# Spreading filler matmuls, moving casts and halving the first transposes in an attention and MLP kernel

## Chip, cores, metric

One core of a Trainium2 chip. The metric is the device time of one execution in microseconds (us).

## The reference

```python
x = A_x                                    # 1 x 2048 x 512, bf16
xn = _layernorm(x)
q = xn @ wq                                # 32 heads of 128
k, v = last 512 rows of k_cache, v_cache   # 8 kv heads, each for 4 q heads
o = softmax(q @ k.T * 128**-0.5) @ v       # no mask
s = o @ wo                                 # 4096 -> 512
g = silu(silu(xn @ w1) @ w2)               # 512 -> 1792 -> 512
return x + s * g
```

## The kernel before

The 2048 tokens are worked in 4 blocks of 512, and each block in 32 steps, one per head: 128 steps, numbered s. In step s TensorE computes four score tiles for head s, q for head s + 2 and P times V for head s - 4. Block 0 fills the rest of each step with the MLP matmuls of all four blocks ("fillers"), blocks 1 to 3 with the output projection of the block before. The last projection is done in a tail with fewer, combined products. Every engine's order is the program's order. A **unit** is a group of matmuls that sum into one bank of PSUM, the memory that TensorE writes to here; ScalarE or VectorE has to read the bank out before the next unit can use it. Fillers that stand together between two other matmuls are called a **clump**.

```python
PS_BUFS = {"sc": 4, "q": 1, "o": 1, "f": 2}        # PSUM banks

# MLP unit: 4 matmuls into one of the two f banks, then tanh on ACT, then one pass on DVE
if c == 0:
    cur["ps"] = ps.tile([P, BLK], FP32, name="h_ps", tag=tag_of(f), bufs=PS_BUFS[tag_of(f)])
h_mm(cur["ps"], b, f, c, 0, BLK)
if c == ND - 1:
    h_evac(cur["ps"], b, f)        # th = tanh(0.5 h) on ACT; hT = (th + 1) * h on DVE

# q: one bank, emptied by a cast
if b == NBLK - 1 and h % 2 == 1:
    nc.scalar.copy(qT[s], cur["ps"])
else:
    nc.vector.tensor_copy(qT[s], cur["ps"])

# P V: one bank, emptied on DVE
cur["ps"] = ps.tile([P, BLK], FP32, name="o_ps", tag="o", bufs=1)

# one step
cut = spread(n)                    # how many fillers at each of six places
score(s, 0)
if s >= 1:
    normalise(s - 1, 2, 3)
    flip(s - 1)
for u in qu[:2]: u()
pump(cut[0])
for u in qu[2:]: u()
pump(cut[1])
score(s, 1)
for u in pu[:2]: u()
pump(cut[2])
for u in pu[2:]: u()
pump(cut[3])
score(s, 2)
normalise(s, 0, 1)
pump(cut[4])
score(s, 3)
pump(cut[5])
# then, one tile per step: stats of blocks 2 and 3 in steps 2-5 and 8-11,
# centring and transposing them in steps 7-10 and 14-17
...
# start: layer norm of tiles 0 and 1, then PE transposes
stats(0, 0); stats(0, 1)
rstd_first(0); center(0, 0); rstd_first(1); center(0, 1)
nc.scalar.activation(scratch, scratch, ACT.Tanh)      # loads the tanh table
warm_up(10)
t0 = turn(0); keep(nc.vector, t0, 0); warm_up(1)
t1 = turn(1); keep(nc.vector, t1, 1); warm_up(1)
```

(Line breaks of short loops are joined here.)

The softmax here doesn't subtract the row's maximum and nothing guards it: scores larger than these inputs give would overflow.

Of the kernel before, what the change touches and what calls it, by code (L numbers as in the profile page):

```python
# [9 lines left out]
P = 128  # L10
ALU = mybir.AluOpType
# [11 lines left out]
def kernel(  # L23
# [28 lines left out]
    FH = NFC // 2  # L52
    HALF = BLK // 2
    HP = HQ // 2

    x2 = A_x.flatten_outer_dims()
    out2 = out.flatten_outer_dims()
# [145 lines left out]
    def q_units(s, tag="q"):  # L203
        b, h = divmod(s, HQ)
        cur = {}

        def mm(c):
            if c == 0:
                cur["ps"] = ps.tile([P, BLK], FP32, name="q_ps", tag=tag, bufs=1)
            nc.tensor.matmul(  # L210
                cur["ps"],
                wq_sb[h // REP][:, c, (h % REP) * DH : (h % REP + 1) * DH],
                xnT[b][:, c, :],
                start=(c == 0),
                stop=(c == ND - 1),
            )
            if c == ND - 1:
                qT[s] = work.tile([P, BLK], BF16, name="qT", bufs=3)
                if b == NBLK - 1 and h % 2 == 1:
                    nc.scalar.copy(qT[s], cur["ps"])  # L220
                else:
                    nc.vector.tensor_copy(qT[s], cur["ps"])  # L222

        return [lambda c=c: mm(c) for c in range(ND)]
# [40 lines left out]
            out=s25[p].rearrange("p a b -> p (a b)"), in0=o[:, 0, :], in1=o[:, 1, :], op=ALU.add  # L265
        )

    def pv_units(s):
        b, h = divmod(s, HQ)
        cur = {}  # L270

        def mm(kc):
            if kc == 0:
                cur["ps"] = ps.tile([P, BLK], FP32, name="o_ps", tag="o", bufs=1)
            nc.tensor.matmul(  # L275
                cur["ps"], v_sb[h // REP][:, kc, :], pT[s][:, kc, :], start=(kc == 0), stop=(kc == NKC - 1)
            )
            if kc == NKC - 1:
                if s % 2 == 0:
                    oT[s // 2] = work.tile([P, 2, BLK], BF16, name="oT", tag="oT", bufs=OT_BUFS // 2)  # L280
                nc.vector.tensor_copy(oT[s // 2][:, s % 2, :], cur["ps"])  # L281
                if b == NBLK - 1 and s % 2 == 1:
                    row_sums(h // 2)
                del pT[s], p_all[s], qT[s], den[s]

        return [lambda kc=kc: mm(kc) for kc in range(NKC)]
# [38 lines left out]
    def out_units(b):  # L325
        acc = {}
        xes = {}

        def mm(j, h):
            t = b * BLKT + j  # L330
            if h == 0:
                acc[j] = ps.tile([P, D], FP32, name="s_ps", tag="f", bufs=2)
            nc.tensor.matmul(  # L333
                acc[j],
                oT[(b * HQ + h) // 2][:, h % 2, j * P : (j + 1) * P],
                wo_of(h),
                start=(h == 0),
                stop=(h == HQ - 1),
            )
            if h == HQ // 2:  # L340
                xes[j] = reg.tile([P, D], BF16, name="x_e", tag=f"pair{4 + j % 2}")
                nc.gpsimd.dma_start(xes[j], x2[ds(t * P, P), :])
            if h == HQ - 1:
                xe = xes[j]
                sg = reg.tile([P, D], FP32, name="sg", tag=f"pair{2 + j % 2}")
                nc.vector.tensor_tensor(out=sg, in0=acc[j], in1=g_sb[b][:, j, :], op=ALU.mult)
                nc.vector.scalar_tensor_tensor(  # L347
                    out=xe, in0=sg, scalar=0.25, in1=xe, op0=ALU.mult, op1=ALU.add
                )
                nc.gpsimd.dma_start(out2[ds(t * P, P), :], xe)  # L350

        return [lambda a=a: mm(*a) for a in out_order()]



# [76 lines left out]
    def tail():  # L432
# [42 lines left out]
        def bank(tag, shape, name):  # L475
            return ps.tile(shape, FP32, name=name, tag=tag, bufs=PS_BUFS[tag])
# [44 lines left out]
        for t in range(2):  # L521
            group(3, t, "sc")
            run(3, t, EARLY)
            for u in pv_units(NSTEP - LAG + t):
                u()
            for p in range(3 * t, 3 * t + 3):
                diag(p)
# [10 lines left out]
            run(5, t, EARLY)  # L538
        for p in range(8):
            skew(p)  # L540
        for u in pv_units(NSTEP - 1):
            u()
        for p in (14, 15):
            diag(p)
# [4 lines left out]
        for t in range(2):  # L549
            run(4, t, (HP - 2,))  # L550
            run(5, t, (HP - 2,))
        m2 = bank("q", [P, 2, HALF], "m2_ps")
        for p in EARLY:
            mm(m2[:, 0, :], 2, p, 0)
        for t in range(2):
# [54 lines left out]
    with tc.manual_schedule(engines={ENG.PE, ENG.Activation, ENG.DVE, ENG.SP, ENG.Pool}):  # L610
# [21 lines left out]
        def warm_up(n):  # L632
            for _ in range(n):
                nc.tensor.matmul(warm_ps, warm[:, 0:P], warm, start=True, stop=True)

        def turn(j):
            t_ps = ps.tile([P, ND, P], BF16, name="t_ps", tag="qo"[j % 2], bufs=1)
            for c in range(ND):
                nc.tensor.transpose(t_ps[:, c, :], x_blk[0][:, j, c * P : (c + 1) * P], ident)
            return t_ps  # L640

        def keep(eng, t_ps, j):
            dst = xnT[0][:, :, j * P : (j + 1) * P]
            (nc.scalar.copy if eng is nc.scalar else nc.vector.tensor_copy)(dst, t_ps)

        stats(0, 0)
        stats(0, 1)
        rstd_first(0)
        center(0, 0)
        rstd_first(1)  # L650
        center(0, 1)
        nc.scalar.activation(scratch, scratch, ACT.Tanh)
        warm_up(10)
        t0 = turn(0)
        keep(nc.vector, t0, 0)
        warm_up(1)
        t1 = turn(1)
        keep(nc.vector, t1, 1)
        warm_up(1)
        stats(0, 2)  # L660
        stats(0, 3)
        rstd_of(2, 2)
# [26 lines left out]
        for i in range(2 * FH):  # L689
            h_pair(i, i // FH)  # L690
            if i == 3:
                t2 = turn(2)
                t3 = turn(3)
                keep(nc.scalar, t2, 2)
                keep(nc.vector, t3, 3)
            if i >= 2 * FH - 4:
                stats(1, i - 2 * FH + 4)
            if i in (2 * FH - 3, 2 * FH - 2):
                k = i - 2 * FH + 3
                for u in q_units(k, "qo"[k]):  # L700
                    u()
# [26 lines left out]
        }  # L728
        sums = col_sums()

        def spread(n):

            cut = [n // 6] * 6
            for k in (5, 4, 1, 3, 0, 2)[: n % 6]:
                cut[k] += 1
            return cut if n != 4 else (0, 0, 0, 0, 2, 2)

        n_more = 4 * LAG
        wo_first = False
        for s in range(NSTEP):  # L740
            b, h = divmod(s, HQ)
            if b >= 1 and h == 0:
                assert done >= n_mlp or b > 1
                fill += out_units(b - 1)
            n = 4
            if b == 0:
                n = min(4 * (h + 1), n_more) + (h + 1) * (n_mlp - n_more) // HQ - done
            cut = spread(n)
            qu = q_units(s + 2) if s + 2 < NSTEP else []
            pu = pv_units(s - LAG) if s >= LAG else []  # L750
            score(s, 0)
            if s >= 1:
                normalise(s - 1, 2, 3)
                flip(s - 1)
            for u in qu[:2]:
                u()
            pump(cut[0])
            for u in qu[2:]:
                u()
            pump(cut[1])  # L760
            score(s, 1)
            for u in pu[:2]:
                u()
            pump(cut[2])
            for u in pu[2:]:
                u()
            pump(cut[3])
            score(s, 2)
            normalise(s, 0, 1)
            pump(cut[4])  # L770
            score(s, 3)
            if s == NSTEP - 1:
                normalise(s, 2, 3)
                flip(s)
            pump(cut[5])
            while sums and sums[0][0] <= s:
                sums.pop(0)[1]()
            for b2, s0 in ((2, 2), (3, 8)):
                if s0 <= s < s0 + BLKT:
                    stats(b2, s - s0)  # L780
                if s == s0 + BLKT - 1:
                    rstd_of(b2 * BLKT, BLKT)
            if s < 2:
                for j in (2 * s, 2 * s + 1):
                    center(1, j)
                    flip_x(1, j)
            for b2, s0 in ((2, 7), (3, 14)):
                if s0 <= s < s0 + BLKT:
                    center(b2, s - s0)
                    flip_x(b2, s - s0)  # L790
            if s % REP == 1 and s < HQ and s // REP + 2 < HKV:
                load_kq(s // REP + 2)
                load_v(s // REP + 2)
            if not wo_first and done >= n_mlp - BLKT * NFC:
                new_wo("big0")
                new_wo("big1")
                wo_first = True
            if s == HQ:
                for tag in ("big2", "big3", "pair0", "pair1"):
                    new_wo(tag)  # L800
            for args in wo_plan.get(s, []):
                load_wo(*args)
# [29 lines left out]
```

## Time and profile before

Before the change: 552.18 us, median of 4 runs (551.7 to 552.33). In the profile PE is TensorE, PEld its weight loads, DVE is VectorE, ACT is ScalarE and POOL is GpSimd. The page of the profiled run: the span; then busy time of each engine, its share of the span and its instructions; then the chain of work that ended last.

```profile
span 550.0 us, 8480 instructions
...
PE 541.0 (98%) x2628; PEld 261.6 (48%) x2676; DVE 458.5 (83%) x1261; ACT 389.0 (71%) x1122; POOL 20.6 (4%) x41
...
PE 93%; DVE 3%; ACT 1%; issue 1%; DMA 1%
```

TensorE is the bound. (48 of its 2676 matmul records are missing in this trace.) But "98%" cannot tell what is left, since the ends of matmuls are modelled and overlap. The starts can: back to back, 128x512 matmuls start 0.216 us apart and 128x256 ones 0.109 us. The Trainium skill ("TensorE: Matmul & The Clock Gate", Part 1) gives N / 2.4 GHz + 2.5 ns, which agrees. The program has 2324, 336 and 16 matmuls of 512, 256 and 128 columns; at that spacing they take some 539.4 us. **A slot**, in what follows, is one spacing of 0.216 us, and **a hole** is how much later than the spacing a matmul starts.

The view of waits, TensorE's alone (engine, line, what it waited for, us in total, times, longest):

```profile
PE warm_ps L634 <- DVE eps L73: 1.2, 1, 1.2
PE q_ps L210 <- DVE qT L222: 0.7, 1, 0.7
PE h_ps L676 <- DVE xnT L644: 0.3, 1, 0.3
PE o_ps L275 <- DVE oT L281: 0.2, 1, 0.2
PE t_ps L639 <- DVE x L122: 0.2, 1, 0.2
```

This view counts from the modelled end of the matmul before, which lies 0.16 us after the next start that was due (0.38 against 0.216 us), so it shows 0.65 us of a hole of 0.81, and the 0.11 us that it leaves of a hole of 0.28 is not listed at all. The starts show 0.81 us at q_ps, 0.36 us at o_ps, and in block 0 a further 1.5 us at h_ps and oB_ps, none of which is in the list. One of those, in the timeline (start, duration, engine, line, operation, count, and in brackets the idle time before and what ended it):

```profile
148.92 0.59 PE L146 MATMUL h_ps<-xnT,w 128*128 128x512 bf16 x2
149.34 0.60 ACT L156 ACTIVATE th<-h_ps 128x512 bf16<-128x512 f32 x1 [0.61 <-PE h_ps L146]
149.57 0.59 PE L146 MATMUL h_ps<-xnT,w 128*128 128x512 bf16 x2
149.97 0.69 DVE L157 SCALAR_TENSOR_TENSOR hT<-th,h_ps 128x512 bf16<-128x512 bf16 x1 [0.15 <-ACT th L156]
150.22 0.87 PE L146 MATMUL h_ps<-xnT,w 128*128 128x512 bf16 x2
```

Two back-to-back matmuls show 0.59 us together; the last pair shows 0.87, so its second one came 0.28 us late, at 150.71. It is the first matmul of a unit and needs the bank that the matmul at 148.92 filled last. Tanh and the DVE pass follow each other without queueing, and the bank is free at 150.66. The round trip of a bank, from the start of its last matmul to its next use, is thus 150.71 - 148.92 = 1.79 us. In between lie seven slots of 0.216 us, 1.51 us, because fillers come in pairs at the end of a step. The difference is the hole.

### The profile page before, as it was taken

Reading aid. Unit: us, or ns where it says so; the run is one execution under the profiler, and the core shown is the slowest. Engines: PE = TensorE matmul, PEld = TensorE weight load, DVE = VectorE, ACT = ScalarE, POOL = GpSimd, SP = SyncE. Lnnn points to the kernel's source line nnn. Section 1 sums busy time; section 2 is a strip of 40 time slices with the busy share of each in tenths; the row PEclk is TensorE's granted clock in tenths of the full one; section 3 lists DMA queues with packets and bytes.
Section 4 is the critical chain, followed back from the end, with each engine's and each line's share of the span. In section 5 each row is a group of like instructions: output and inputs, shape, how many; then the busy total and the mean of one; then the engine's idle time right before and its main releaser. Section 6 shows DMA issues by size and latency. Waiting matters only on the chain.

```text
span 550.0 us, 8480 instructions
## 1 busy us (share of the span) xinstructions
PE 541.0 (98%) x2628; PEld 261.6 (48%) x2676; DVE 458.5 (83%) x1261; ACT 389.0 (71%) x1122; POOL 20.6 (4%) x41
## 2 busy tenths in 40 slices
PE   8999999999999999999999999999999999999997
PEld 5644444444444444444444444444444444444586
DVE  6869978976886688898889888988898889988887
ACT  4658756766775677777777777777788888788600
POOL 1000100000000100010001000100010000000010
PEclk9999999999999999999999999999999999999999
DMA  9969779769749799979887988798879877987921
GB/s 286 250 114 182 155 152 153 155 144 178 147 79 204 161 214 223 205 147 189 164 151 145 189 164 144 155 188 161 153 150 184 156 150 152 183 153 154 172 78 39
DMA packets 297837, 89.69 MB, mean 163 GB/s; under 512 B 282304, under 2 KB 296896, under 8 KB 297792
## 3 DMA queue, kind: packets, MB, share of 16 engines
q1 hardware_dynamic: 296064, 85.09, 77.9%
q0 software_dynamic: 1312, 3.67, 2.7%
q8 instruction: 21, 0.34, 0.2%
q10 hardware_dynamic: 416, 0.39, 0.2%
q14 instruction: 24, 0.20, 0.1%
HBM read 17.30 MB, written 2.10 MB: 35 GB/s over the span
## 4 chain that ended last, share of the span: by engine, by line
PE 93%; DVE 3%; ACT 1%; issue 1%; DMA 1%
PE sc_ps L232 19%; PE q_ps L210 19%; PE o_ps L275 19%; PE s_ps L333 14%; PE oB_ps L179 9%; PE h_ps L146 6%; PE m_ps L473 4%; PE h_ps L676 2%; DVE p_all L247 1%; ACT p_all L235 1%; ACT th L156 1%; DMA x<-in_A_x_dram 1%; DVE oT L281 0%; DVE hT L157 0%; DVE x_e L347 0%
## 5 line engine op out<-in xcount | busy, mean ns | idle before, releaser
L235 ACT ACTIVATE p_all<-sc_ps 128x512 bf16<-128x512 f32 x512 | 305.4, 597 | 104.0 <-PE sc_ps L232 102.0
L232 PE MATMUL sc_ps<-kT,qT 128*128 128x512 bf16 x512 | 193.7, 379 | 0.7
L247 DVE TENSOR_SCALAR p_all<-p_all,rden 128x512 bf16<-128x512 bf16 x512 | 157.9, 351 | 9.1
L210 PE MATMUL q_ps<-xnT,wq 128*128 128x512 bf16 x498 | 134.4, 379 | 1.1 <-DVE qT L222 0.7
L275 PE MATMUL o_ps<-pT,v 128*128 128x512 bf16 x496 | 133.6, 379 | 0.7 <-DVE oT L281 0.2
L281 DVE CAST oT<-o_ps 128x512 bf16<-128x512 f32 x128 | 88.3, 689 | 41.2 <-PE o_ps L275 38.7
L235 ACT ACTIVATION_READ_ACCUMULATOR p_all<-sc_ps 128x1 f32 x512 | 100.7, 197 | 0.0
L333 PE MATMUL s_ps<-wo_big,oT 128*128 128x512 bf16 x327 | 98.0, 379 | 0.5
L232 PEld LDWEIGHTS <-qT 128*128 128x128 bf16 x512 | 50.1, 98 | 61.3 <-issue 1.4
L210 PEld LDWEIGHTS <-wq 128*128 128x128 bf16 x512 | 50.1, 98 | 60.9 <-issue 1.2
L275 PEld LDWEIGHTS <-v 128*128 128x128 bf16 x512 | 50.1, 98 | 59.9 <-issue 0.4
L222 DVE CAST qT<-q_ps 128x512 bf16<-128x512 f32 x112 | 76.9, 687 | 1.6 <-PE q_ps L210 1.1
L179 PE MATMUL oB_ps<-w,hT 128*128 128x512 bf16 x220 | 64.6, 379 | 0.3
L333 PEld LDWEIGHTS <-oT 128*128 128x128 bf16 x384 | 37.6, 98 | 45.3
L146 PE MATMUL h_ps<-xnT,w 128*128 128x512 bf16 x164 | 50.1, 379 | 0.6
L245 DVE RECIPROCAL rden<-den 128x2 f32<-128x2 f32 x256 | 40.4, 158 | 10.8 <-ACT p_all L235 10.8
L179 PEld LDWEIGHTS <-hT 128*128 128x128 bf16 x224 | 21.9, 98 | 26.4
L157 DVE SCALAR_TENSOR_TENSOR hT<-th,h_ps 128x512 bf16<-128x512 bf16 x42 | 28.7, 683 | 4.6 <-ACT th L156 4.6
L156 ACT ACTIVATE th<-h_ps 128x512 bf16<-128x512 f32 x42 | 25.1, 598 | 9.1 <-PE h_ps L146 9.1
L146 PEld LDWEIGHTS <-w 128*128 128x128 bf16 x168 | 16.4, 98 | 20.2 <-issue 0.7
L189 DVE SCALAR_TENSOR_TENSOR gate<-th,oB_ps 128x512 bf16<-128x512 bf16 x16 | 11.0, 687 | 13.8 <-ACT th L188 13.8
L350 POOL DMA_DIRECT2D out_dram<-x_e x12 | 6.6, 549 | 314.5 <-DVE rden L245 258.2
(63 smaller groups left out, 235.9 us busy)
## 6 DMA issues: line engine op xcount, KB each, us to landing
wq<-in_A_wq_dram SPq DMA_DIRECT2D x8, 512.0 KB, 4.3
w<-in_B_w_dram SPq DMA_DIRECT2D x3, 896.0 KB, 9.9
pT<-p_all SPq DMA_TRANSPOSE x128, 4.4
wo_big<-in_A_wo_dram SPq DMA_DIRECT2D x4, 512.0 KB, 4.6
x<-in_A_x_dram SPq DMA_DIRECT2D x3, 512.0 KB, 8.6
wo_big<-in_A_wo_dram SPq DMA_DIRECT2D x4, 384.0 KB, 4.6
x_e<-in_A_x_dram POOLq DMA_DIRECT2D x12, 128.0 KB, 3.0
out_dram<-x_e POOLq DMA_DIRECT2D x12, 128.0 KB, 2.2
```

The source lines that it names most:

```text
L146: nc.tensor.matmul(h_ps[:, lo : lo + n], w1_sb[f // FH][:, c, (f % FH) * P : (f % FH + 1) * P], xnT[b][:, c, lo : lo + n], start=(c == 0), ...
L156: nc.scalar.activation(th, h_ps, ACT.Tanh, scale=0.5)
L179: nc.tensor.matmul(cur["ps"], hT[b][f // 2][:, f % 2, j * P : (j + 1) * P], w2_sb[f // FH][:, f % FH, :], start=(f == 0), stop=(f == NFC - 1),
L210: nc.tensor.matmul(cur["ps"], wq_sb[h // REP][:, c, (h % REP) * DH : (h % REP + 1) * DH], xnT[b][:, c, :], start=(c == 0), stop=(c == ND - 1),
L222: nc.vector.tensor_copy(qT[s], cur["ps"])
L232: nc.tensor.matmul(sc, qT[s][:, j * P : (j + 1) * P], kT[h // REP], start=True, stop=True)
L235: nc.scalar.activation(p_all[s][:, :, j, :], sc.rearrange("p (kc q) -> p kc q", q=P), ACT.Exp, scale=INV_SQRT_DH, accum_out=den[s][:, j : ...
L245: nc.vector.reciprocal(rden, den[s][:, j0 : j1 + 1])
L247: nc.vector.tensor_scalar_mul(p_all[s][:, :, j, :], p_all[s][:, :, j, :], rden[:, j - j0 : j - j0 + 1])
L275: nc.tensor.matmul(cur["ps"], v_sb[h // REP][:, kc, :], pT[s][:, kc, :], start=(kc == 0), stop=(kc == NKC - 1))
L281: nc.vector.tensor_copy(oT[s // 2][:, s % 2, :], cur["ps"])
L333: nc.tensor.matmul(acc[j], oT[(b * HQ + h) // 2][:, h % 2, j * P : (j + 1) * P], wo_of(h), start=(h == 0), stop=(h == HQ - 1),)
```

## The change

It makes the tile order of TensorE smoother and takes single waits away. The matmuls are the same. Its core:

```diff
 # q cast of the last block
-                if b == NBLK - 1 and h % 2 == 1:
+                if b == NBLK - 1 and (h % 2 == 1 or h in busy):
                     nc.scalar.copy(qT[s], cur["ps"])
+    busy = {i // 4 + 3 for i, (_, h) in enumerate(out_order()) if h == HQ - 1}
 # tail: P V sums take turns between two banks
-            for u in pv_units(NSTEP - LAG + t):
+            for u in pv_units(NSTEP - LAG + t, "oq"[t]):
-        for u in pv_units(NSTEP - 1):
+        for u in pv_units(NSTEP - 1, "q"):
-        m2 = bank("q", [P, 2, HALF], "m2_ps")
+        m2 = bank("o", [P, 2, HALF], "m2_ps")
 # start: halves, tile 0 copied by ACT, tanh table later
-        center(0, 0)
+        center_half(0, 0)
+        center_half(0, 1)
         rstd_first(1)
-        center(0, 1)
-        nc.scalar.activation(scratch, scratch, ACT.Tanh)
+        center_half(1, 0)
+        center_half(1, 1)
         warm_up(10)
-        t0 = turn(0)
-        keep(nc.vector, t0, 0)
-        warm_up(1)
-        t1 = turn(1)
-        keep(nc.vector, t1, 1)
-        warm_up(1)
+        for j in range(2):
+            for k in range(2):
+                turn_half(j, k)
+                keep_half(nc.vector.tensor_copy if j else nc.scalar.copy, j, k)
+                if k:
+                    warm_up(1)
+        nc.scalar.activation(scratch, scratch, ACT.Tanh)
 # block 0: one filler after each other unit (blocks 1 to 3 keep their order)
+                units = S[0:1] + qu + S[1:2] + pu[:2] + S[2:3] + pu[2:] + S[3:4]
+                for i, u in enumerate(units):
+                    u()
+                    pump((i + 1) * n // len(units) - i * n // len(units))
 # stats and centring of blocks 2 and 3
-            for b2, s0 in ((2, 2), (3, 8)):        # stats, one tile a step
+            for b2, s0 in ((2, 8), (3, 18)):       # two tiles in the step, two at its end
-            for b2, s0 in ((2, 7), (3, 14)):       # centring, one tile a step
+            for b2, s0 in ((2, 9), (3, 19)):       # two tiles a step
 ... (bodies cut)
```

The busy set is {17, 18, 33, 34}; 17 was on ACT already and heads end at 31, so one cast moves: that of head 18. Before, most of block 2's stats and of block 3's centring stood in steps in which h units run (first MLP matmul, units of 4); now all of both blocks' stand in steps in which the second MLP matmul runs, whose units are 14 matmuls long.

More of the change, by code (lines that the diff above doesn't have):

```diff
@@ L54 @@
     HP = HQ // 2
+    HP4 = P // 2
     x2 = A_x.flatten_outer_dims()
@@ L266, in row_sums, with pv_units @@
         )
-    def pv_units(s):
+    def pv_units(s, tag="o"):
         b, h = divmod(s, HQ)
@@ L273, in mm @@
             if kc == 0:
-                cur["ps"] = ps.tile([P, BLK], FP32, name="o_ps", tag="o", bufs=1)
+                cur["ps"] = ps.tile([P, BLK], FP32, name="o_ps", tag=tag, bufs=1)
             nc.tensor.matmul(
@@ L634, in warm_up, with turn_half, keep_half, center_half @@
                 nc.tensor.matmul(warm_ps, warm[:, 0:P], warm, start=True, stop=True)
+        def turn_half(j, k):
+            tag = "qoff"[2 * j + k]
+            t_first[j, k] = ps.tile([P, 2, P], BF16, name="t_ps", tag=tag, bufs=PS_BUFS[tag])
+            for c in range(2):
+                lo = (2 * k + c) * P
+                nc.tensor.transpose(t_first[j, k][:, c, :], x_blk[0][:, j, lo : lo + P], ident)
+        def keep_half(copy, j, k):
+            cs = slice(2 * k, 2 * k + 2)
+            copy(xnT[0][:, cs, j * P : (j + 1) * P], t_first[j, k])
+        def center_half(j, k):
+            v = x_blk[0][:, j, k * HALF : (k + 1) * HALF]
+            nc.vector.tensor_scalar(
+                out=v, in0=v, scalar1=mv[:, j, 0:1], scalar2=rstd[:, j : j + 1], op0=ALU.subtract, op1=ALU.mult
+            )
         def turn(j):
@@ L640, in turn @@
             return t_ps
-        def keep(eng, t_ps, j):
-            dst = xnT[0][:, :, j * P : (j + 1) * P]
-            (nc.scalar.copy if eng is nc.scalar else nc.vector.tensor_copy)(dst, t_ps)
+        t_first = {}
         stats(0, 0)
@@ L648 @@
         rstd_first(0)
-        center(0, 0)
+        center_half(0, 0)
+        center_half(0, 1)
         rstd_first(1)
-        center(0, 1)
-        nc.scalar.activation(scratch, scratch, ACT.Tanh)
-        warm_up(10)
-        t0 = turn(0)
-        keep(nc.vector, t0, 0)
-        warm_up(1)
-        t1 = turn(1)
-        keep(nc.vector, t1, 1)
-        warm_up(1)
+        center_half(1, 0)
+        center_half(1, 1)
+        warm_up(10)
+        for j in range(2):
[4 more added lines that the diff above has]
+                    warm_up(1)
+        nc.scalar.activation(scratch, scratch, ACT.Tanh)
         stats(0, 2)
@@ L693 @@
                 t3 = turn(3)
-                keep(nc.scalar, t2, 2)
-                keep(nc.vector, t3, 3)
+                nc.scalar.copy(xnT[0][:, :, 2 * P : 3 * P], t2)
+                nc.vector.tensor_copy(xnT[0][:, :, 3 * P : 4 * P], t3)
             if i >= 2 * FH - 4:
@@ L729 @@
         sums = col_sums()
-        def spread(n):
-            cut = [n // 6] * 6
-            for k in (5, 4, 1, 3, 0, 2)[: n % 6]:
-                cut[k] += 1
-            return cut if n != 4 else (0, 0, 0, 0, 2, 2)
         n_more = 4 * LAG
@@ L747, with sc @@
                 n = min(4 * (h + 1), n_more) + (h + 1) * (n_mlp - n_more) // HQ - done
-            cut = spread(n)
             qu = q_units(s + 2) if s + 2 < NSTEP else []
             pu = pv_units(s - LAG) if s >= LAG else []
-            score(s, 0)
-            if s >= 1:
-                normalise(s - 1, 2, 3)
-                flip(s - 1)
-            for u in qu[:2]:
-                u()
-            pump(cut[0])
-            for u in qu[2:]:
-                u()
-            pump(cut[1])
-            score(s, 1)
-            for u in pu[:2]:
-                u()
-            pump(cut[2])
-            for u in pu[2:]:
-                u()
-            pump(cut[3])
-            score(s, 2)
-            normalise(s, 0, 1)
-            pump(cut[4])
-            score(s, 3)
-            if s == NSTEP - 1:
-                normalise(s, 2, 3)
-                flip(s)
-            pump(cut[5])
+            def sc(j):
+                score(s, j)
+                if j == 0 and s >= 1:
+                    normalise(s - 1, 2, 3)
+                    flip(s - 1)
+                if j == 1 and s in (8, 18):
+                    stats(2 + s // 18, 0)
+                    stats(2 + s // 18, 1)
+                if j == 2:
+                    normalise(s, 0, 1)
+                if j == 3 and s == NSTEP - 1:
+                    normalise(s, 2, 3)
+                    flip(s)
+            S = [lambda j=j: sc(j) for j in range(BLKT)]
+            if b == 0:
+                units = S[0:1] + qu + S[1:2] + pu[:2] + S[2:3] + pu[2:] + S[3:4]
+                for i, u in enumerate(units):
+                    u()
+                    pump((i + 1) * n // len(units) - i * n // len(units))
+            else:
+                for u in S[0:1] + qu + S[1:2] + pu + S[2:3]:
+                    u()
+                pump(2)
+                S[3]()
+                pump(2)
             while sums and sums[0][0] <= s:
                 sums.pop(0)[1]()
-            for b2, s0 in ((2, 2), (3, 8)):
-                if s0 <= s < s0 + BLKT:
-                    stats(b2, s - s0)
-                if s == s0 + BLKT - 1:
+            for b2, s0 in ((2, 8), (3, 18)):
+                if s == s0:
+                    stats(b2, 2)
+                    stats(b2, 3)
                     rstd_of(b2 * BLKT, BLKT)
@@ L786 @@
                     flip_x(1, j)
-            for b2, s0 in ((2, 7), (3, 14)):
-                if s0 <= s < s0 + BLKT:
-                    center(b2, s - s0)
-                    flip_x(b2, s - s0)
+            for b2, s0 in ((2, 9), (3, 19)):
+                if s in (s0, s0 + 1):
+                    for j in (2 * (s - s0), 2 * (s - s0) + 1):
+                        center(b2, j)
+                        flip_x(b2, j)
             if s % REP == 1 and s < HQ and s // REP + 2 < HKV:
```

## The prediction

> **What bounds it now.** TensorE. The profile page gives PE 98% busy, but that is modelled, so I counted starts. In the timeline of TensorE, 128x512 matmuls start 0.216 us apart back to back (128x256: 0.109 us), as the Trainium skill states ("TensorE: Matmul & The Clock Gate", Part 1: N / 2.4 GHz + 2.5 ns). The program has 2324 + 336 + 16 matmuls of 512, 256 and 128 columns; at those spacings that is 539.4 us of the 550.0 us span. The rest: 1.2 us before the first matmul, 3.5 us after the last, some 2 us of warm-up matmuls at double spacing, and about 4 us of holes, placed from the starts:
>
> - start: 0.57 us before the first transposes (5.78 us), 0.46 us before the first h matmul (7.60 us, released by the DVE copy of xnT);
> - block 0: holes of 1.5 us in all, at h_ps and oB_ps: 0.27 (42.2 us), 0.20 (110.5), three of 0.28 (150.7, 156.2, 161.6), three of 0.06. The two f banks were still held by tanh (ACT 0.60 us) and the DVE pass (0.69 us);
> - last block: 0.81 us at 468.26 us, q_ps waiting for the DVE cast of qT, which stood behind the output evacuation (0.68 + 0.69 us);
> - tail: 0.36 us at 522.39 us, o_ps waiting for the DVE cast of oT.
>
> 188 to 460 us: none.
>
> **What the change does.** The same 2676 matmuls, almost the same DVE and ACT work. Only holes can go.
>
> 1. Start: centring and transposing in halves, copies of tile 0 on ACT, tanh table load (1.28 us) after them. From the DVE 128x512 centring (0.41 us) and copy (0.42 us), ACT copy (0.58 us), I estimate halves of 0.28 / 0.28 / 0.38 us; the first h matmul starts near 7.0 us instead of 7.6. Some is lost again at the transposes of tiles 2 and 3: their centring ended at 11.07 us, just as PE came (11.09 us), and moves forward only about 0.3 us. Gain 0.45 us (0.2 to 0.6).
> 2. Block 0: fillers are spread singly, and stats and centring of blocks 2 and 3 leave the h phases. The three 0.28 us holes come from clumps of filler at the step's end; I expect them gone, those at 42 and 110 us partly. Gain 0.9 us (0.2 to 1.4).
> 3. Block 3: qT of head 18 on ACT, which idles 0.39 us there. Gain 0.8 us.
> 4. Tail: PV alternates between banks o and q. Gain 0.35 us.
>
> All lie on the critical path: PE has no slack. Sum 2.5 us; less 0.2 us for new small holes: 2.3 us, 0.4%.
>
> **Predicted: 549.9 us**, 8 in 10 between 548.9 and 551.4. Chances: faster by over 2% 0.01, within 2% 0.98, slower by over 2% 0.01.
>
> **What would show it right or wrong.** First h matmul at about 7.0 us; no wait of q_ps near 465 us, none of o_ps near 520 us; holes in block 0 under 0.7 us in sum; PE's last start near 544 us (now 546.27); still 3.5 us after it.
>
> **What would make it wrong.** The last score of a step and the first of the next now stand two matmuls apart: tanh queues behind both exps, and where an h unit ends there a new 0.3 us hole per step would eat point 2. Or the late table load delays the first h evacuations. Or point 1 vanishes in waits of the transposes.

## The result

After the change: 549.76 us, median of 9 runs (549.66 to 549.95), against 551.98 us for 13 runs of before (551.7 to 552.45). The ratio is 0.9960, with a 95% interval of 0.995 to 0.9969. (Ratios are the mean time of one kernel's fast runs over that of the other's of the same rounds, so not quite the ratio of the medians quoted.)

The page after:

```profile
span 547.5 us, 8487 instructions
...
PE 539.4 (99%) x2628; PEld 260.9 (48%) x2676; DVE 458.6 (84%) x1262; ACT 391.9 (72%) x1125; POOL 20.5 (4%) x41
...
PE 97%; DVE 1%; issue 1%; DMA 0%; ACT 0%
```

DVE and ACT did almost the same work. TensorE's waits after, the whole list:

```profile
PE warm_ps L638 <- DVE eps L74: 1.2, 1, 1.2
PE t_ps L645 <- DVE x L653: 0.7, 1, 0.7
```

The waits of q_ps and o_ps are gone. To see where the time went I cut each trace at starts that every kernel has: the first DVE statistics, the first h matmul, the first score, the first output projection matmul (the beginning of block 1), the last score, the last matmul. In us:

| kernel | first stats to first h | first h to first score | block 0 | blocks 1 to 3 | tail | first h to last matmul |
|---|---|---|---|---|---|---|
| before | 4.08 | 14.41 | 167.87 | 327.58 | 28.80 | 538.66 |
| after | 3.67 | 14.49 | 166.87 | 326.77 | 28.44 | 536.58 |
| difference | -0.41 | +0.08 | -1.00 | -0.81 | -0.36 | -2.08 |

The timeline of TensorE, ACT and DVE after, at the place in block 0 shown above:

```profile
149.39 0.38 PE L147 MATMUL h_ps<-xnT,w 128*128 128x512 bf16 x1
149.81 0.60 ACT L157 ACTIVATE th<-h_ps 128x512 bf16<-128x512 f32 x1 [0.39 <-PE h_ps L147]
150.64 0.68 DVE L158 SCALAR_TENSOR_TENSOR hT<-th,h_ps 128x512 bf16<-128x512 bf16 x1
...
151.55 0.38 PE L147 MATMUL h_ps<-xnT,w 128*128 128x512 bf16 x1
```

From the last matmul of one unit to the first of the next but one there are now ten slots, 2.16 us. The DVE pass even queued for 0.2 us, and the bank was free in time, at 151.32.

The 0.08 us lost before the first score are two holes of 0.04 us: at 10.18 us, just after the second half of w1 had landed (10.13), and at 13.72 us, where the first h matmul of tiles 2 and 3 waited for tile 3's copy (DVE, 13.24 to 13.66 us).

Two holes are left in block 0, of 0.27 and 0.18 us. Their lines stand with the experiment that removes them.

### The profile page after: what moved, and what is told of

It is laid out like the page before. It is cut to its first block, busy times and chain, and to the rows that moved or that the text cites. A ratio compares the mean times of both kernels' runs of the same rounds, so it can differ in the third digit from the quotient of the medians.

```text
span 547.5 us, 8487 instructions
## 1 busy us (share of the span) xinstructions
PE 539.4 (99%) x2628; PEld 260.9 (48%) x2676; DVE 458.6 (84%) x1262; ACT 391.9 (72%) x1125; POOL 20.5 (4%) x41
## 3 DMA queue, kind: packets, MB, share of 16 engines
q0 software_dynamic: 1312, 3.67, 2.5%
## 4 chain that ended last, share of the span: by engine, by line
PE 97%; DVE 1%; issue 1%; DMA 0%; ACT 0%
PE sc_ps L233 20%; PE o_ps L276 20%; PE q_ps L211 20%; PE s_ps L334 15%; PE oB_ps L180 9%; PE h_ps L147 6%; PE m_ps L477 4%; PE h_ps L696 2%; DMA x<-in_A_x_dram 0%; DVE st L109 0%; DVE hT L158 0%; DVE p_all L248 0%; PE t_ps L645 0%; DVE gate L190 0%; ACT th L189 0%
## 5 line engine op out<-in xcount | busy, mean ns | idle before, releaser
L211 PE MATMUL q_ps<-xnT,wq 128*128 128x512 bf16 x499 | 144.7, 379 | 0.4
L276 PE MATMUL o_ps<-pT,v 128*128 128x512 bf16 x498 | 142.9, 379 | 0.7
L180 PE MATMUL oB_ps<-w,hT 128*128 128x512 bf16 x218 | 78.4, 379 | 0.2
L147 PE MATMUL h_ps<-xnT,w 128*128 128x512 bf16 x163 | 61.4, 379 | 0.2
```

Of the source, the lines that this page charges most:

```text
L147: nc.tensor.matmul(h_ps[:, lo : lo + n], w1_sb[f // FH][:, c, (f % FH) * P : (f % FH + 1) * P], xnT[b][:, c, lo : lo + n], start=(c == 0), ...
L180: nc.tensor.matmul(cur["ps"], hT[b][f // 2][:, f % 2, j * P : (j + 1) * P], w2_sb[f // FH][:, f % FH, :], start=(f == 0), stop=(f == NFC - 1),
L211: nc.tensor.matmul(cur["ps"], wq_sb[h // REP][:, c, (h % REP) * DH : (h % REP + 1) * DH], xnT[b][:, c, :], start=(c == 0), stop=(c == ND - 1),
L276: nc.tensor.matmul(cur["ps"], v_sb[h // REP][:, kc, :], pT[s][:, kc, :], start=(kc == 0), stop=(kc == NKC - 1))
```

## The experiments

Each run changes the kernel before, or where said the kernel after. The same cuts of all traces, in us (bold: what differs from the parent kernel by over 0.05; the first column scatters and is treated apart):

| kernel | stats to h | h to score | block 0 | blocks 1 to 3 | tail | h to last | time, median | before |
|---|---|---|---|---|---|---|---|---|
| p_start | 3.80 | 14.44 | 167.87 | 327.59 | 28.80 | 538.70 | 551.90 | 551.93 |
| p_spread | 3.95 | **14.70** | **168.74** | 327.57 | 28.80 | 539.81 | 553.12 | 551.93 |
| p_stats | 3.69 | 14.41 | **167.77** | 327.58 | 28.79 | 538.56 | 552.24 | 551.93 |
| p_cast | 3.69 | 14.41 | 167.87 | **326.77** | 28.79 | 537.85 | 550.97 | 551.93 |
| p_tail | 3.69 | 14.41 | 167.87 | 327.58 | **28.44** | 538.30 | 551.45 | 551.83 |
| x_phase | 3.75 | 14.41 | **167.57** | 327.57 | 28.80 | 538.36 | 551.61 | 551.83 |
| x_sums | 3.99 | 14.41 | 167.87 | **326.77** | 28.79 | 537.84 | 551.38 (1 run) | 551.90 |
| s_act | 3.79 | 14.41 | 167.89 | 327.57 | 28.79 | 538.66 | 552.07 (1 run) | 551.90 |
| s_halves | 3.75 | **14.52** | 167.86 | 327.57 | 28.79 | 538.73 | 551.93 (1 run) | 551.90 |
| c_after (= after) | 3.66 | 14.50 | 166.87 | 326.77 | 28.45 | 536.59 | 549.76 | 551.83 |
| b_phase (from after) | 3.67 | 14.49 | **166.42** | 326.77 | 28.45 | 536.12 | 549.38 | 551.83 |
| b_start (from after) | 3.78 | **14.41** | **166.42** | 326.77 | 28.45 | 536.04 | 549.23 | 551.90 |

A stage after the first column that a run leaves alone repeats to 0.02 us (on different chips), while the ratios of five timed runs have intervals of some 0.13%, 0.7 us, either way.

### The start alone

The start of the diff above, nothing else.

> The kernel before with the new start alone (halves, copies of tile 0 on ACT, late tanh table load). My theory: the holes of TensorE add up, so the first h matmul starts at 7.1 us (before: 7.60, after: 7.10) and the last matmul starts 0.4 to 0.5 us earlier than the 546.27 of before; the holes at 42, 110, 151 to 162, 468 and 522 us stay (about 0.5 us earlier each). Time about 0.45 us below before. Rival: TensorE reaches the transposes of tiles 2 and 3 too early, or the holes of block 0 grow by what the start gave; then the last matmul starts within 0.15 us of 546.27.

The time did not move: 0.9998 (0.9984 to 1.0011). In the profile the first h matmul came at 7.23 us and the last matmul at 545.93, 0.34 us earlier than in that of before, which looks nearly like the theory. But the first h matmul comes as early with the old start in other runs: 7.08, 6.98, 7.09, 7.07 and 7.21 us in p_stats, p_cast, p_tail, x_phase and p_spread (7.47 in x_sums). My theory fell, and the 7.60 us of the profile of before was a slow instance. The timeline tells why. First before, in the profile that the prediction was made from, then p_stats, whose start is the same code:

```profile
5.78 0.61 PE L639 MATMUL t_ps<-ident,x 128*128 128x128 bf16 x4 [0.15 <-DVE x L122]
...
7.60 0.60 PE L676 MATMUL h_ps<-xnT,w 128*128 128x256 bf16 x4 [0.30 <-DVE xnT L644]
```

```profile
5.65 0.40 PE L639 MATMUL t_ps<-ident,x 128*128 128x128 bf16 x4 [0.23 <-DVE x L122]
...
7.08 1.14 PE L676 MATMUL h_ps<-xnT,w 128*128 128x256 bf16 x9 [0.30 <-DVE xnT L644]
```

The same first four transposes took 0.61 us in one run and 0.40 in the other. TensorE starts slow (the warm-up matmuls start 0.427 us apart) and comes to full rate (0.216 us) at a moment that varies: near 4.0 us in p_cast, near 6.8 us in the profile of before, where most of the eight transposes were still slow. The Trainium skill ("TensorE: Matmul & The Clock Gate", Part 1) explains such a moment by a free-running activity window that does not begin with the kernel; the spread seen here is in the closing list. In the seven profiles with the old start, 3.69 us from the first statistics to the first h matmul go with full rate before 5.2 us, 3.75 with 5.9 (x_phase), and 3.95, 3.99 and 4.08 with 6.3, 6.6 and 6.8 (p_spread, x_sums, before). (The moments are the packed trace's, and the starts agree.) No run set that moment, so this is an order seen and not an experiment. Where the transposes ran at full rate throughout, the old start took 3.69 us from the first statistics to the first h matmul (p_stats, p_cast, p_tail) and the new one 3.67 (after, b_phase).

### Halves alone, and the copy on ACT alone

```diff
 # s_halves: the new start, but
-                keep_half(nc.vector.tensor_copy if j else nc.scalar.copy, j, k)
+                keep_half(nc.vector.tensor_copy, j, k)
 # and the tanh activation before warm_up(10), as it was
 # s_act: the old start, but
-        keep(nc.vector, t0, 0)
+        keep(nc.scalar, t0, 0)
 # and the tanh activation behind the copies
```

> The kernel before with the halves alone: centring, transposes and copies in halves, all copies on DVE, tanh table load where it was. Theory (DVE bounds the start): DVE now has the halves' extra 0.4 us and all copies, so 3.8 to 4.1 us from the first statistics to the first h matmul even at full rate, worse than the old start's 3.69. Rival (shorter hand-over is what counts, as my prediction had it): 3.3 to 3.6 us.

> The kernel before with one thing of the new start: tile 0's copy, whole, goes to ACT, and the tanh table load behind it; centring, transposes and the copy of tile 1 stay whole. So far the old start took 3.69 to 4.08 us from the first DVE statistics to the first h matmul, the new one 3.66 to 3.80, the long ones where the warm-ups came late to full rate. Theory (DVE bounds the start: halving centring costs DVE about 0.2 us per tile, as much as the copy on ACT saves): here DVE keeps the saving without the cost, so 3.5 to 3.6 us where the transposes run at full rate. Rival (PE's order of transposes and warm-ups bounds it): 3.69 or more.

Halves gave 3.75 us and the copy on ACT 3.79, so neither was better than the old start at full rate, 3.69. Both of my theories missed, and so did the rival of s_halves; the rival of s_act (3.69 or more) held. What the traces show of the terms: a half of the centring takes 344 ns against 408 ns for the whole (128x256 and 128x512, view of the line), far from half, so halving costs DVE 0.28 us per tile in summed durations (the two halves overlap: from first start to last end they take 0.60 us). My prediction had put a half at 0.28 us.

In s_act the copy of tile 1 waited 0.49 us for its transposes, so DVE's saving was not needed: the copy ended 3.64 us after the first statistics, as in p_stats. The h matmul came 0.15 us after that copy's end, against 0.05 us in p_stats. The weight loads show where the 0.10 us went: in p_stats the load for this matmul starts at 6.40 us, long before the copy's end at 7.03; in s_act it starts at 7.22, after the end at 7.11. The packed trace has a separate wait instruction of TensorE just before the load there, as in every run here that copies tile 0 on ACT and tile 1 on DVE; those with both on DVE have none.

In s_halves DVE worked with hardly a gap (under 0.05 us) from the first centring to the last copy (5.18 to 7.28 us), so there it did bound the start, only at 3.75 us and not the 3.8 or more of my theory.

### Fillers spread singly, alone

The block 0 loop of the diff, with stats and centring where they were.

> The kernel before with single spreading of the fillers alone; stats and centring stay where they were. Theory A (round trip): an f bank is free again 1.79 us after the start of the last matmul that filled it (0.38 matmul, 0.60 tanh, 0.69 DVE, the rest handovers, where nothing queues), so a hole is 1.79 us minus 0.216 us for each matmul between that last one and the next use of the bank: 7 slots in clumps give the 0.28 us holes, 9 to 10 slots singly give none. Then the three holes of 0.28 us near 151 to 162 us are gone with this part alone, and the sum of holes in block 0 falls from 1.5 to about 0.5 us; time about 1.0 us below before. Theory B (DVE load): the holes come from stats and centring that stood in the h phases; then most of the 1.5 us stays.

Neither theory. The three holes of 0.28 us near 151 to 162 us are gone, as theory A said. But the kernel got slower: 1.0019 (1.0006 to 1.0032), block 0 by 0.87 us. The hole of 0.28 us at 42 us stays, and new holes of 0.32, 0.62, 0.62, 0.29 and 0.22 us stand at 45.6, 51.4, 57.2, 109.9 and 113.6 us. The timeline at the second:

```profile
48.63 0.38 PE L146 MATMUL h_ps<-xnT,w 128*128 128x512 bf16 x1
...
49.12 0.60 ACT L156 ACTIVATE th<-h_ps 128x512 bf16<-128x512 f32 x1
49.16 0.69 DVE L108 BATCH_NORM_STATS2 st<-x 128x6 f32<-128x512 bf16 x1
...
50.14 0.62 DVE L247 TENSOR_SCALAR p_all<-p_all,rden 128x512 bf16<-128x512 bf16 x2
...
50.67 0.68 DVE L157 SCALAR_TENSOR_TENSOR hT<-th,h_ps 128x512 bf16<-128x512 bf16 x1
...
51.41 0.38 PE L146 MATMUL h_ps<-xnT,w 128*128 128x512 bf16 x1 [0.46 <-DVE hT L157]
```

Tanh was ready at 49.72, but the pass that frees the bank began at 50.67, behind the statistics of block 2 and the normalising of the step before. DVE works in program order (the Trainium skill, same page, Part 1, on queue depths: strict FIFO), and the trace agrees: the pass waited from 49.72 to 50.67 us behind work that stands ahead of it. From 48.63 to 51.41 are 2.78 us; ten slots cover 2.16.

The extra 0.29 us before the first score is another thing. The second half of w1 is needed 28 matmuls, 3.06 us, after the first h matmul. Here that was 10.27 us, it landed at 10.50, and TensorE went on at 10.54. So what an earlier first h matmul gains can be lost again at this load. It landed at 10.02 us in before, 10.13 in after, and between 9.70 (p_start) and 10.50 over all runs.

### Stats and centring moved, alone

> The kernel before with stats and centring of blocks 2 and 3 moved as in the change, fillers in clumps as before. Theory A: the three holes of 0.28 us near 151 to 162 us stay, that of 0.20 near 110 us stays within 0.1; block 0 still has 1.2 to 1.6 us of holes, time within 0.3 us of before. Theory B (DVE load): the sum of holes in block 0 falls to about 0.5 us and the time by about 1 us.

As theory A said: four holes of 0.27 to 0.28 us and the one of 0.21 stay, block 0 gains 0.10 us, and the time does not move: 1.0001 (0.9988 to 1.0013). So the two parts together are not the sum of each: +0.87 and -0.10 alone, -1.00 together. Spreading removes the round-trip holes but then fails on the DVE queue; moving the DVE work removes that, which alone was hardly a hole.

### The clumps kept, the phase changed

```diff
-        n_more = 4 * LAG
+        n_more = 8
```

With 8 extra fillers at the beginning instead of 16, every step from the third on has exactly 12.

> The kernel before with one constant changed: 8 instead of 16 extra fillers in the first steps, so that each later step takes exactly 12 fillers and each h unit of four ends with the second, fourth or sixth clump. Clumps, stats and centring stay. Theory A (round trip of 1.79 us): from the last matmul of a unit to the next use of its bank there are now 10 or more slots, 2.16 us, so the holes of 0.28 us near 151 to 162 us and that of 0.27 near 42 us go although the clumps stay; block 0 has at most 0.5 us of holes (what is left by stats in the DVE queue), time about 1 us below before. Rival (my prediction's words: the clumps at the step's end make the holes): the 0.28 us holes stay, one per step.

The holes of 0.28 us and the one at 42 us went, though the clumps stayed. So the rival, which were my prediction's words, is wrong: a clump does no harm by itself, but where it stands in the unit does. The size of the gain was missed, since three new holes of 0.33 us came at 44.9, 50.4 and 55.9 us, in the steps with block 2's stats (view of waits, TensorE):

```profile
PE h_ps L146 <- DVE hT L157: 0.5, 3, 0.2
```

Block 0 gained 0.30 us; the time, 0.9994 (0.9981 to 1.0006), does not resolve it.

### The phase changed in the kernel after

The same line in the changed kernel, with the changed kernel again as control.

> The changed kernel with the same constant at 8: every step of block 0 has 12 fillers and h units end at the 4th, 8th or 12th filler. Theory A: the two holes left in block 0 of the changed kernel (0.27 us at 41.5 and 0.18 us at 111.4) go, the first because the fillers there are no longer two to each other matmul, the second because no h unit ends just after a step's first score, where its tanh stood behind two exps. First h matmul to last matmul 536.1 us (changed kernel: 536.58); time 0.3 to 0.5 us below the changed kernel of the same call. Rival: the holes only move to other steps, same sum within 0.1.

> The changed kernel again, as control on the same chip: 0.9955 to 0.997 of the time before; first h matmul to last matmul 536.6 us within 0.1; the first h matmul itself at 6.9 to 7.6 us, since the earlier runs suggest that it moves from run to run with the DMA and with the moment at which the warm-up matmuls come to full rate, whichever start the kernel has.

The two holes left were these in the timeline of after. At 41.51 us, hidden in the last pair's 0.87:

```profile
39.73 0.38 PE L180 MATMUL oB_ps<-w,hT 128*128 128x512 bf16 x1
...
40.14 0.60 ACT L189 ACTIVATE th<-oB_ps 128x512 bf16<-128x512 f32 x1 [1.84 <-PE oB_ps L180]
...
40.77 0.69 DVE L190 SCALAR_TENSOR_TENSOR gate<-th,oB_ps 128x512 bf16<-128x512 bf16 x1 [0.15 <-ACT th L189]
...
41.02 0.87 PE L147 MATMUL h_ps<-xnT,w 128*128 128x512 bf16 x2
```

and at 111.41 us:

```profile
109.06 0.38 PE L147 MATMUL h_ps<-xnT,w 128*128 128x512 bf16 x1
...
109.42 0.59 ACT L236 ACTIVATE p_all<-sc_ps 128x512 bf16<-128x512 f32 x1
...
109.99 0.60 ACT L157 ACTIVATE th<-h_ps 128x512 bf16<-128x512 f32 x1
...
110.67 0.68 DVE L158 SCALAR_TENSOR_TENSOR hT<-th,h_ps 128x512 bf16<-128x512 bf16 x1
...
111.41 0.38 PE L147 MATMUL h_ps<-xnT,w 128*128 128x512 bf16 x1
```

The first is the plain round trip, 41.51 - 39.73 = 1.78 us: in the first four steps there is no P V, and the fillers stand too densely. The second is the queue: tanh could have begun at 109.44, had to let the exp of the step's first score go first, and began at 109.99.

With the constant at 8, both are gone: no hole of over 0.02 us from block 0 to the last matmul, and block 0 at 166.42 us. The time is 549.38 us (549.18 to 549.44), against 549.76 (549.69 to 550.44) for the control: 0.38 us less, and no run of one lies in the range of the other. Against before, 0.9952 (0.994 to 0.9965). This beats both kernels.

### The cast of head 18 alone, and the sums moved instead

p_cast has the first lines of the diff (busy), nothing else. x_sums leaves the casts alone and begins one group of column sums of the last block later:

```diff
-            s0 = 110 + 4 * i
+            s0 = 110 + 4 * i + 2 * (i == 0)
```

> The kernel before with qT of head 18 of the last block on ACT alone. Theory: the hole of 0.81 us at 468 us is gone and no other comes in the last block, so the last matmul starts 0.8 us earlier (545.45); time about 0.8 us below before. Rival: ACT, now with two qT casts running, holds the score banks longer and part of the 0.81 us comes back at the next scores; then a hole of over 0.2 us appears within 10 us after.

> The kernel before with the first of the four column-sum groups of the last block begun two steps later (about 7 us), all casts left on DVE. Theory: the 0.81 us hole at 468 us comes of a DVE queue that the output evacuation (0.68 + 0.69 us) only overfills because a sum of 0.68 us and one of 0.55 us stand in it in the same two steps; blocks 1 and 2 have the same evacuation and no hole. Then the hole falls below 0.2 us with no cast moved, and no other over 0.2 us comes. Rival (the evacuation alone, as my prediction said): a hole of 0.5 us or more stays near 468 us.

Both remove all of the 0.81 us, and both bring blocks 1 to 3 to 326.77 us. p_cast measured 0.9983 (0.9971 to 0.9996). Before, the q bank was full at about 465.0 us, and the timeline of DVE and TensorE shows what the cast waited for:

```profile
465.00 0.68 DVE L346 TENSOR_TENSOR sg<-s_ps,gate 128x512 f32<-128x512 f32 x1
...
465.72 0.69 DVE L347 SCALAR_TENSOR_TENSOR x_e<-sg,x_e 128x512 bf16<-128x512 f32 x1
...
466.33 0.55 DVE L378 TENSOR_TENSOR wq_sum<-wo_big 128x768 bf16<-128x768 bf16 x1
...
467.52 0.69 DVE L222 CAST qT<-q_ps 128x512 bf16<-128x512 f32 x1
...
468.26 1.02 PE L210 MATMUL q_ps<-xnT,wq 128*128 128x512 bf16 x4 [0.65 <-DVE qT L222]
```

And x_sums, where the same evacuation stands in the queue but no sum:

```profile
464.34 0.68 DVE L346 TENSOR_TENSOR sg<-s_ps,gate 128x512 f32<-128x512 f32 x1
465.06 0.69 DVE L347 SCALAR_TENSOR_TENSOR x_e<-sg,x_e 128x512 bf16<-128x512 f32 x1
...
466.39 0.68 DVE L222 CAST qT<-q_ps 128x512 bf16<-128x512 f32 x1
...
467.31 0.38 PE L210 MATMUL q_ps<-xnT,wq 128*128 128x512 bf16 x1
```

So the output evacuation alone makes no hole. It was the sums (0.68 us in the step before, 0.55 us here) that overfilled DVE's queue. Putting one cast on ACT, which had 0.39 us idle there, is one cure, and starting the sums two steps later is another.

### The tail alone

> The kernel before with the tail's PV sums alternating between banks o and q, nothing else. Theory: the hole of 0.36 us at 522 us goes and nothing else changes; from the first h matmul to the last matmul of all 538.3 us (before: 538.66). Time about 0.35 us below before, which five rounds may just not resolve. Rival: TensorE only meets the next wait of the tail earlier (pT of the last heads, or DVE), and a new hole of like size appears behind.

As expected: tail 28.44 against 28.80 us, time 0.999 (0.9977 to 1.0002), which by itself does not exclude no change. The timeline before, and then after:

```profile
521.66 0.68 DVE L281 CAST oT<-o_ps 128x512 bf16<-128x512 f32 x1
521.71 0.49 PE L473 MATMUL m_ps<-wq_sum,oT 128*128 128x256 bf16 x3
522.39 1.02 PE L275 MATMUL o_ps<-pT,v 128*128 128x512 bf16 x4 [0.19 <-DVE oT L281]
```

```profile
519.41 0.68 DVE L282 CAST oT<-o_ps 128x512 bf16<-128x512 f32 x1
519.47 0.49 PE L477 MATMUL m_ps<-wq_sum,oT 128*128 128x256 bf16 x3
519.79 1.03 PE L276 MATMUL o_ps<-pT,v 128*128 128x512 bf16 x4
```

After, the P V sums begin while DVE still empties the other bank.

### The best order with a plainer start

b_phase with the start of s_act in place of the halves.

> The changed kernel with 8 extra fillers and with the start of s_act in place of the halves. Theory: no hole in blocks 0 to 3, and 0.1 us off the start where TensorE then does not wait for the second half of w1, which landed at 9.8 to 10.5 us and is needed 3.06 us after the first h matmul; so 549.2 to 549.4 us where the run with the halves had 549.38, too little for a verdict against that one; ratio to before 0.994 to 0.9965. Rival (halves are better): first h matmul over 3.75 us after the first statistics.

549.23 us (549.14 to 550.01), 0.9954 (0.994 to 0.9967). Its first h matmul came later after the statistics than with the halves (3.78 against 3.67 us), which the rival said and not my theory, but from there to the first score it lost nothing (14.41 against 14.49). The sums, 18.19 and 18.16 us, are equal within the scatter. In these two profiles the halves bring nothing; TensorE was at full rate before 5.7 us in both.

## Why the prediction was right or wrong

The total was right: 549.9 us foreseen, 549.76 measured. The terms were not all right.

- **What bounds it, and that only holes can go**: right. First h to last matmul fell by 2.08 us, the sum of the stages' holes, and the timed medians by 2.22 us (2.07 in the control).
- **Point 4, the tail, 0.35 us**: right, 0.36 us, shown by p_tail.
- **Point 3, the cast, 0.8 us**: size right, 0.81 us, shown by p_cast. The cause as I put it, that the cast "stood behind the output evacuation", was half of it: x_sums shows that the column sums had to be there too.
- **Point 2, block 0, 0.9 us**: size right, 1.00 us. The step that failed is "the three 0.28 us holes come from clumps of filler at the step's end". The runs put in its place the round trip of a bank, 1.79 us, against the slots until its next use: x_phase removes the same holes with the clumps kept. I also took the moved stats for a side matter, but without them the spreading costs 0.87 us (p_spread). The holes at 42 and 110 us, which I expected to go in part, stayed nearly whole: 0.27 and 0.18 us, of 0.27 and 0.20. The danger I named, tanh behind exps, is what made one of the two, 0.18 us (behind one exp, not two); the other, 0.27 us, is a plain round trip.
- **Point 1, the start, 0.45 us**: wrong. Alone it measured 0.03 us, with an interval that excludes a gain of over about 0.9 us but not 0.45, so the cuts have to decide: at full rate 3.67 us against 3.69 (0.02 us gained), and 0.03 to 0.09 us lost again before the first score. The term was mis-sized because I read it off one profile. In that profile TensorE came to full rate later than in most, and I took its 7.60 us for the kernel's own. The profiles of before and after differ by 0.41 us in that column, which looks like the predicted 0.45, but the old start showed 3.69 us three times.
- That the total came out is luck in part: errors of opposite sign. The start did not give its 0.45 us; against that, of the 0.2 us taken off for new holes only 0.08 came, and block 0 gave 0.1 us more. By the cuts the gain is 2.08 us and by the timed medians 2.22, against 2.3 foreseen.

Open: how much the new start helps where TensorE comes late to full rate. With full rate near 6 us it took 3.66 us (c_after), against 3.75 with the old start (x_phase); near 6.5 us 3.80 (p_start), against 3.95 to 4.08 at 6.3 to 6.8. These are two instances against four, so the 0.02 us holds only for an early full rate, and 0.1 to 0.2 us is my estimate from them for a late one.

## What to carry to other kernels

Where one engine is busy throughout, count its holes from the starts of its instructions, not from busy shares or the list of waits, and cut the trace into stages: an untouched stage here repeats to 0.02 us, which finds effects that the time cannot. A PSUM bank's round trip (last matmul, evacuations, hand-overs, 1.79 us here) must fit into the slots before its next use, and everything that stands ahead of the evacuation in an in-order queue adds to it, so spreading the matmuls and clearing the evacuating engine's queue have to be done together. Do not size a term at the start of a kernel from a single profile.

## What the Trainium skill lacked or had wrong

- "TensorE: Matmul & The Clock Gate", Part 1: the moment of full rate is said to vary by 0.5 us either way, though a note in the same Part tells of one kernel with 6, 11 or 14 slow matmuls. Over these runs it lay between about 4.0 us (p_cast) and 6.8 us (before) after the span's start, with the first matmul at 1.18 us each time. That fits the note and not the 0.5 us. The first h matmul came up to 0.39 us later after the first statistics at equal work (before against p_stats).
- "ScalarE: Activation LUTs", What ACT_TABLE_LOAD costs: a load of 1.283 us and a drain of 1.38 us for each switch to a different set of tables. The load took 1.28 us here, but no such drain is seen: in after ACT's copies ended at 6.60 us, the load began at 6.61 and the tanh behind it at 7.91. ScalarE copies did run ahead of the load under the table of sqrt, as the section on table sets says of copies.
- No page has the round trip of a matmul bank through tanh and one VectorE pass: 1.78 to 1.79 us without queueing for 128x512 fp32, of which 0.38 are the last matmul, 0.60 tanh and 0.69 VectorE.
